# Moving 26 score maxima from the short sections to the front of a fused spectral-mix and attention kernel

## The chip, the cores and the metric

The kernel runs on one core of a Trainium2 chip. A core has a matrix engine (TensorE, PE in the profile, with its weight loads shown as PEld), a vector engine (VectorE, DVE), a scalar engine (ScalarE, ACT), GpSimd (POOL) and SyncE (SP), which here only issues transfers. They run at the same time, each through its own instructions in order, and wait for each other through semaphores. PE writes to PSUM, eight banks of 128 x 512 floats; ACT and DVE read them, GpSimd works on SBUF alone in this kernel.

The metric is the time of one execution in device microseconds (us), the median of several runs.

## The reference

For one input x (2048 x 512) the output is g * a + (1 - g) * b, with a gate per row, a two-dimensional Fourier transform a (its real part, by matrices), and attention b with 32 heads of 16 columns:

```python
g = sigmoid((x * gate_w).sum(-1, keepdims=True))
# a
ar = einsum("bsd,ed->bse", x, dft_hid_re);  ai = einsum("bsd,ed->bse", x, dft_hid_im)
a  = einsum("ts,bse->bte", dft_seq_re, ar) - einsum("ts,bse->bte", dft_seq_im, ai)
# b
q, k, v = split(x @ wqkv)                    # 32 heads of 16
p = softmax(q @ k^T * 16 ** -0.5)            # 2048 x 2048 for each head
b = (p @ v) @ wo
```

The inputs make the scores large, so softmax needs the maximum of each row of scores before the exponentials.

## The kernel before

Products are made in a rounded 32-bit type. Where precision matters a matrix is held as two parts, a rounded high part and a low part (the rest), and a product is the sum of three: high by high, high by low, low by high. `hi_lo` makes the parts: ACT copies the source into the high part, then DVE (or GpSimd, where the call says so and the source is in SBUF) subtracts.

Two heads form a *stack*: the high and low parts of q and k of a head lie in 64 partitions of `qs[p % 2]` and `ks[p % 2]`, the second head in the other 64. There are 16 stacks; two lie on the chip at a time. `load_stacks(p, heads)` (L267) fetches one from DRAM: for each head two fills with zeros and six rows of parts for p = 1 and 2, fewer fills later.

Scores are made twice. Once with the queries as rows, for their maxima: `a_tile(i, h)` (L288) makes one product of 128 queries by 512 keys for head h of stack i // 64, in a bank of PSUM (an "a"), and DVE reduces it to 128 maxima (L296). Each stack has 64 such i, each for two heads; 2048 maxima in all. When half a stack is done, `m_parts` and `m_rows` turn the maxima into two more rows of the queries, by way of DRAM. Then the scores proper, `scores(u, qb, h)` (L784, an "s"), come with the keys as rows and the maximum already subtracted; ACT makes the exponentials into `pt` (L801). A unit u is 128 keys by 1024 queries of one stack, four scores; there are 512 units. `pv` (L834) multiplies a unit with its values: four narrow products side by side, into the bank `acc`.

PE uses only 64 of its 128 rows for an "a" or an "s". The kernel therefore runs a second stream of products in the other 64 rows at the same time: products of the Fourier transform or of the output projection, each cut into two halves.

**The front.** First q and k (to 93 us), then v, then `b`, the imaginary half of the hidden transform. `pairs_of` (L400) makes the last eight tiles of v and all 16 tiles of b in groups of four. A group has four *phases* (L378): two pairs of tiles, each with its first and then its second half. A phase has 12 places, in each a half product of one tile beside one of the other; with `maxima` set, in places 3 and 9 two maxima (both heads) are put in between, which takes one more place. The first of the 24 phases makes none, 22 make four, until `a_next` has reached LEAD = 44. The second maximum of place 9 uses the bank `acc`, the others three banks in turn. When a pair has its second half, `done` empties it: `v_done` (L356) copies the two heads' columns into `vt`, one with ACT, one with DVE; `b_done` (L367) makes high and low parts in a tile `hl` of four buffers, stores them to `b_d` through SP, and for the first four tiles also makes the parts of the next weights (`wre`), the low ones on GpSimd.

**The main loop.** `segment` (L954) reads a pattern, one word for each place. "a" and "s" are a maximum and a score, with the number of the PSUM bank (0 to 6; 6 is `acc`), "-" is neither; a word with one letter also issues one half product of the second stream, a word with two letters puts two of the first kind side by side, and "|" is `pv` of one unit. There are two start sections (START), 13 pairs of short ones (THIN, 12 products of the second stream), 96 pairs of full ones (FULL, 16 products) and 13 pairs at the end (NINE, 9 products). A section pair makes the first half of its second-stream products, then the second half.

Before each section `run_plan` runs what is due: the plan (L882) is a list by units of values done. `load_stacks` for stack 1 is due at 0, the start of the loop; for stack p from 2 on the first head at 32 * (p - 1), the second two units later. The maxima of the main loop go on from `lead`, where the front stopped.

In the front, behind the transfers of `load_stacks`, SP issues the stores of `b_done`; in the main loop SP also issues the loads of the raw sequence matrices (`c_load`, L441), two buffers in turn, and the stores of values.

Of the kernel before, what the change touches and what calls it, by code (L numbers as in the profile page):

```python
# [9 lines left out]
F32 = mybir.dt.float32  # L10
F32R = mybir.dt.float32r
AF = mybir.ActivationFunctionType
ALU = mybir.AluOpType
AX = mybir.AxisListType

P = 128
S = 2048
D = 512
H = 32
DH = 16  # L20
NP = H // 2
KT = D // P
NT = S // P
UNITS = NP * 32
LEAD = 44
RAW = 6
PSUM = bass.MemoryType.PSUM
DRAM = bass.MemoryType.DRAM
# [3 lines left out]
def mix_kernel(ctx: ExitStack, tc: tile.TileContext, xa_t, xa, wqkv, w_hid, w_seq, wo, gate_w, out):  # L32
# [5 lines left out]
    nc = tc.nc  # L38
# [4 lines left out]
    used = list(range(7))  # L43
# [58 lines left out]
    acc = psO.tile([P, 512], F32, "acc")  # L102

    def hi_lo(hi, lo, src, lo_eng=None):
        nc.scalar.copy(hi, src)
        (lo_eng or nc.vector).tensor_tensor(lo, src, hi.bitcast(F32), ALU.subtract)
# [7 lines left out]
    st1 = right.__enter__()  # L114
# [9 lines left out]
    def staged(src):  # L124
        raw = st1.tile([P, D], F32, name="raw", bufs=RAW)
        i = nc.sync.dma_start(raw, src)
        if behind:
            tc.add_manual_dep(i.ins, behind.pop().ins.name,
                              mybir.DependencyInfo(mybir.DependencyClass.Sync, mybir.DependencyReason.DATA))
        return raw  # L130
# [58 lines left out]
    def bank():  # L189
        nonlocal banks  # L190
        banks += 1
        return (psS if banks % 2 else psA).tile([P, 512], F32, name="s" if banks % 2 else "a")


    with tc.tile_pool(name="qk", bufs=1, reuse_waits="tile") as pool:
# [38 lines left out]
        for tb in range(4):  # L234
# [4 lines left out]
            for c in range(2):  # L239
# [12 lines left out]
                for ct in range(4):  # L252
                    ps = bank()
# [9 lines left out]
    vt = main.tile([P, NT, NP, 33], F32, name="vt")  # L263
# [3 lines left out]
    def load_stacks(p, heads=range(2)):  # L267
        q_t, k_t = qs[p % 2], ks[p % 2]
        for h in heads:
            rows = slice((2 * p + h) * DH, (2 * p + h + 1) * DH)  # L270
            o = 64 * h
            if p:
                n = 64 if p < 3 else 50
                nc.sync.dma_start(q_t[o + 48:o + n].bitcast(F32), z_d[:n - 48])
                if p < 3:
                    nc.sync.dma_start(k_t[o + 50:o + 64].bitcast(F32), z_d[:14])

            for i, (qv, kv) in enumerate(((0, 0), (0, 1), (1, 0))):
                part = slice(o + 16 * i, o + 16 * i + 16)
                nc.sync.dma_start(q_t[part].bitcast(F32), qk_d[0][qv, rows])  # L280
                nc.sync.dma_start(k_t[part].bitcast(F32), qk_d[1][kv, rows])
# [6 lines left out]
    def a_tile(i, h, ps=None, bank=None):  # L288
        p, j = divmod(i, 64)
        qt, kb = divmod(j, 4)  # L290
        if ps is None:
            ps = psA.tile([P, 512], F32, "a", bank)
        r = slice(64 * h, 64 * h + (64 if p else 48))
        nc.tensor.matmul(ps, qs[p % 2][r, qt * P:(qt + 1) * P], ks[p % 2][r, kb * 512:(kb + 1) * 512],  # L294
                         start=True, stop=True)
        user = nc.vector.tensor_reduce(mx[p % 2][:, h, qt, kb:kb + 1], ps, AX.X, ALU.max)  # L296
        hf = j // 32
        a_left[p, hf] = a_left.get((p, hf), 64) - 1
        if not a_left[p, hf]:
            deferred.extend((partial(m_parts, p, hf), partial(m_rows, p, hf)))  # L300
        return user
# [45 lines left out]
    a_next = 0  # L347

    def x_mm(s, wh, wl):

        t = xab[s // 4][:, s % 4]
        for kt in range(KT):
            h1, l1 = (t[:, v, kt * P:(kt + 1) * P] for v in range(2))
            yield from ((h1, wh[kt]), (h1, wl[kt]), (l1, wh[kt]))

    def v_done(s, ps):  # L356
        pv = ps.rearrange("p (r h d) -> p r h d", h=2, d=DH)
        nc.scalar.copy(vt[:, s, :, 0:16], pv[:, :, 0])
        nc.vector.tensor_copy(vt[:, s, :, 17:33], pv[:, :, 1])
        if s in range(6, 14, 2):  # L360
            kt = (s - 6) // 2
            wt = st1.tile([P, 2, D], F32R, name="hl", bufs=4)
            hi_lo(wt[:, 0], wt[:, 1], wos.pop(0), nc.gpsimd)
            nc.sync.dma_start(wo_d[kt], wt.bitcast(F32))
            wrs.append(staged(w_hid[0, :, kt]))

    def b_done(s, ps):  # L367
        bt = st1.tile([P, 2, D], F32R, name="hl", bufs=4)
        hi_lo(bt[:, 0], bt[:, 1], ps)
        nc.sync.dma_start(b_d[s], bt.bitcast(F32))  # L370
        if s < KT:
            hi_lo(wre[0][s], wre[1][s], wrs.pop(0), nc.gpsimd)
# [3 lines left out]
    made, user = 0, None  # L376

    def phase(pair, half, maxima):  # L378
        nonlocal a_next, user
        before, user = user, None  # L380
        for j in range(12):
            for x, (ps, ops, done) in enumerate(pair):
                st, mv = ops[j]
                r = slice(64 * (half ^ x), 64 * (half ^ x) + 64)
                i = nc.tensor.matmul(ps, st[r], mv[r], start=not half and not j, stop=half == 1 and j == 11)  # L385
                if not j and not x and half:
                    tc.add_manual_dep(i.ins, before.ins.name,
                                      mybir.DependencyInfo(mybir.DependencyClass.Sync, mybir.DependencyReason.DATA))
            if maxima and j in (3, 9):
                for h in range(2):  # L390
                    used = a_tile(a_next, h, acc if h and j == 9 else None)
                user = user or used
                a_next += 1
        if half:
            for ps, ops, done in pair:
                done(ps)
        if deferred:
            deferred.pop(0)()

    def pairs_of(tiles, wh, wl, done):  # L400
        nonlocal made
        tiles = list(tiles)
        for i in range(0, len(tiles), 4):
            new = []
            for s in tiles[i:i + 4]:
                ps = psD.tile([P, 512], F32, name="d") if s % 4 == 1 else psS.tile([P, 512], F32, name="s")
                new.append((ps, list(x_mm(s, wh, wl)), partial(done, s)))
            for half in range(2):
                for pair in (new[:2], new[2:]):
                    phase(pair, half, 0 < made and a_next < LEAD)  # L410
                    made += 1

    for s in range(8):
        ps = psS.tile([P, 512], F32, name="s")
        ops = list(x_mm(s, *wv))
        for i, (st, mv) in enumerate(ops):
            nc.tensor.matmul(ps, st, mv, start=not i, stop=i == len(ops) - 1)  # L417
        v_done(s, ps)
    pairs_of(range(8, NT), *wv, v_done)

    def spare(i, dt, name):
# [4 lines left out]
    wre = [[const.tile([P, D], F32R, name=f"wre{v}{kt}", tag=f"w{4 * v + kt}") for kt in range(KT)] for v in range(2)]  # L426
    ab = [xab[s // 4][:, s % 4] for s in range(NT)]
    pairs_of(range(NT), *([w[:, kt] for kt in range(KT)] for w in (wch, wcl)), b_done)
    run_deferred()
    nc.vector.memset(acc, 0.0)  # L430
    assert a_next == LEAD
    right.__exit__(None, None, None)
# [420 lines left out]
    def take(gen, n, whole=True):  # L853

        got = []
        while len(got) < n:
            x = next(gen, None)
            if x is None:
                break
            x[0].left -= 1  # L860
            got.append((*x, x[0].left == 0))
            if whole and got[-1][4]:
                break
        return got
# [19 lines left out]
    def at(u, f, *args):  # L884
        plan.setdefault(u, []).append(partial(f, *args))
# [9 lines left out]
                    for step, du in enumerate((20, 24, 26)):  # L895
                        at(last + du + 8 * half, block, step, hf, ct, half)

    for p in range(1, NP):
        for h in range(2):
            at(32 * (p - 1) + 2 * h * (p > 1), load_stacks, p, [h])  # L900
    one, two, three = [(psD, "d")], [(psS, "s"), (psD, "d")], [(psS, "s"), (psA, "a"), (psD, "d")]
    side = [(psD, "d"), (psP, "a")]
    at(456, load_yg, 0, range(3))
# [8 lines left out]
    def run_plan(u):  # L912
        for v in sorted(v for v in plan if v <= u + 1):
# [8 lines left out]

    FULL = "a5 s4 a2 s0 a3 s6 a5 s4 s1 s0 s2 a6 a3 a4 s5 a1 | |"
    START = "sA s aS - - a s - - a s - - a", "s a s a s a s a s a s a +s +a"
    THIN = ("a2S4 a1 s3 a0 s6 s2 a4 s3 s1 a6 a0 s5 a2 s4A3 | |",
            "a2S4 a1 s3 a0 s6 s2 a4 s3 s1 a6 a0 s5 a2 s4A3 | |")
    NINE = ("a3 s0 s5 a4 a1 s6 s3 a0 a2 s5A4 | s5S1 a3A0 |",
            "a2S4 a5 s1 a3 s0 s6 a4 a1 s5S2 s0 a3 | s5A4 s1A2 |")

# [75 lines left out]
    def pairs():  # L1005

        for i in range(NT - 3):
            yield THIN, take(hid, 12)
        for i in range(2 * NT * 3):
# [131 lines left out]
```

## Time and profile before

| | us |
|---|---|
| median of 3 runs | 1657.53 (1657.33 to 1657.91) |
| the profiled execution's own time | 1657.73 |
| its span, first to last instruction | 1656.0 |
| granted TensorE clock (mean, of 1) | 0.999 |

The span by stage, from the starts of instructions in the trace:

| stage | from | to |
|---|---|---|
| q, k, and half of v | 0 | 115.2 |
| v and b in pairs, with maxima | 115.2 | 192.5 |
| two start sections | 192.5 | 205.5 |
| 26 short sections | 205.5 | 349.6 |
| 192 full sections | 349.6 | 1451.6 |
| the end | 1451.6 | 1656.0 |

A row of the timeline reads: start, length, engine, line, operation, tile written <- tiles read, shapes, count; in brackets the idle time of the engine before it and what ended it. A row of the view by lines reads: line, engine, operation, tiles, shapes, count, then busy time and the mean length of one in ns, then idle time before it. A row of the stretches gives from:to, length, and for PE, weight loads, DVE, ACT and GpSimd the busy time and the number of instructions. The length shown for one instruction is more than its share of time where the engine overlaps it with the next.

### The profile page before, as it was taken

Reading aid. Unit: us, or ns where it says so; the run is one execution under the profiler, and the core shown is the slowest. Engines: PE = TensorE matmul, PEld = TensorE weight load, DVE = VectorE, ACT = ScalarE, POOL = GpSimd, SP = SyncE. Lnnn points to the kernel's source line nnn. Section 1 sums busy time; section 2 is a strip of 40 time slices with the busy share of each in tenths; the row PEclk is TensorE's granted clock in tenths of the full one; section 3 lists DMA queues with packets and bytes.
Section 4 is the critical chain, followed back from the end, with each engine's and each line's share of the span. In section 5 each row is a group of like instructions: output and inputs, shape, how many; then the busy total and the mean of one; then the engine's idle time right before and its main releaser. Section 6 shows DMA issues by size and latency. Waiting matters only on the chain.

```text
span 1656.0 us, 34484 instructions
## 1 busy us (share of the span) xinstructions
PE 1648.4 (100%) x13082; PEld 990.4 (60%) x13082; DVE 1381.0 (83%) x2362; ACT 1259.6 (76%) x2469; POOL 654.0 (39%) x619
## 2 busy tenths in 40 slices
PE   9999999999999999999999999999999999999998
PEld 7888765555555555555555555555555555544454
DVE  5439888888888888888888888888888888899954
ACT  5212388888888888888788887888888887889996
POOL 0202133443434455444343455544434455333330
PEclk9999999999999999999999999999999999999999
DMA  9973610514151443414157434315141535452014
GB/s 291 348 166 109 186 20 9 70 34 85 46 91 47 74 113 81 95 46 79 47 90 255 92 115 95 87 59 92 47 91 56 116 104 119 139 186 47 25 44 142
DMA packets 85246, 167.16 MB, mean 101 GB/s; under 512 B 22460, under 2 KB 22716, under 8 KB 81068
## 3 DMA queue, kind: packets, MB, share of 16 engines
q1 hardware_dynamic: 84648, 164.30, 39.8%
q8 instruction: 103, 1.69, 0.5%
q10 hardware_dynamic: 432, 0.66, 0.1%
q14 instruction: 63, 0.52, 0.1%
HBM read 109.67 MB, written 55.17 MB: 100 GB/s over the span
## 4 chain that ended last, share of the span: by engine, by line
PE 99%; DMA 0%; DVE 0%; DVEq 0%; ACT 0%; SPq 0%; issue 0%
PE acc L846 28%; PE a L294 22%; PE s L800 19%; PE d L471 12%; PE s L385 3%; PE acc L800 3%; PE acc L294 2%; PE s L417 1%; PE d L385 1%; PE acc L808 1%; PE a L111 1%; PE a L110 1%; PE s L111 1%; PE s L110 1%; PE a L109 1%; PE s L109 1%
## 5 line engine op out<-in xcount | busy, mean ns | idle before, releaser
L296 DVE TENSOR_REDUCE mx<-a 128x1 f32<-128x512 f32 x1808 | 1127.8, 683 | 157.5 <-PE a L294 107.5
L801 ACT ACTIVATE pt<-s 128x512 f32<-128x512 f32 x1792 | 943.9, 628 | 15.1 <-PE s L800 11.1
L294 PE MATMUL a<-ks,qs 64*128 64x512 f32 (+1 forms) x1808 | 673.0, 408 | 0.0
L471 PE MATMUL d<-xab,ch 64*128 64x512 f32 x2016 | 648.1, 396 | 0.0
L800 PE MATMUL s<-qs,ks 64*128 64x512 f32 (+1 forms) x1792 | 591.5, 399 | 0.0
L828 POOL TENSOR_TENSOR oe<-oe,part 128x512 f32<-128x512 f32 x215 | 278.1, 1293 | 659.3 <-ACT part L827 654.3
L846 PE MATMUL acc<-pt,vt 128*17 128x512 f32 x3968 | 479.0, 595 | 0.0
L294 PEld LDWEIGHTS a<-ks,qs 64*128 64x128 f32 (+1 forms) x1808 | 322.2, 184 | 242.6 <-issue 133.1
L471 PE MATMUL d<-xab,cl 64*128 64x512 f32 x1008 | 399.3, 396 | 0.0
L471 PEld LDWEIGHTS d<-xab,ch 64*128 64x128 f32 x2016 | 366.6, 184 | 14.2
L800 PEld LDWEIGHTS s<-qs,ks 64*128 64x128 f32 (+1 forms) x1792 | 320.3, 184 | 81.0 <-ACT pt L801 29.8
L827 ACT COPY part<-acc 128x512 f32<-128x512 f32 x215 | 126.3, 588 | 202.2 <-issue 187.1
L846 PEld LDWEIGHTS acc<-pt,vt 128*17 128x17 f32 x3968 | 89.0, 96 | 228.2 <-issue 148.4
L471 PEld LDWEIGHTS d<-xab,cl 64*128 64x128 f32 x1008 | 185.6, 184 | 6.9
L296 DVE TENSOR_REDUCE mx<-acc 128x1 f32<-128x512 f32 x240 | 165.5, 690 | 11.4
L456 POOL TENSOR_TENSOR cl<-craw,ch 128x512 fp32r<-128x512 f32 x126 | 162.1, 1287 | 10.1
L801 ACT ACTIVATE pt<-acc 128x512 f32<-128x512 f32 x244 | 148.1, 607 | 0.0
L800 PE MATMUL acc<-qs,ks 64*128 64x512 f32 (+1 forms) x244 | 95.4, 391 | 0.0
L294 PE MATMUL acc<-ks,qs 64*128 64x512 f32 (+1 forms) x240 | 94.1, 392 | 0.0
L455 POOL CAST ch<-craw 128x512 fp32r<-128x512 f32 x126 | 77.1, 612 | 18.5 <-PE d L471 14.2
L471 PE MATMUL d<-wre,xab 64*128 64x512 f32 x336 | 83.0, 392 | 0.0
L471 PE MATMUL d<-wo_hl,o_hl 64*128 64x512 f32 x252 | 66.7, 395 | 0.0
(175 smaller groups left out, 1199.4 us busy)
## 6 DMA issues: line engine op xcount, KB each, us to landing
craw<-w_seq SPq DMA_DIRECT2D x128, 256.0 KB
qk<-hl SPq DMA_DIRECT2D x32, 512.0 KB
qs<-qk SPq DMA_DIRECT2D x96, 128.0 KB
ks<-qk SPq DMA_DIRECT2D x96, 128.0 KB
b<-hl SPq DMA_DIRECT2D x16, 512.0 KB
xab<-b SPq DMA_DIRECT2D x16, 512.0 KB
o<-oe SPq DMA_DIRECT2D x62, 128.0 KB
oh<-nh SPq DMA_DIRECT2D x12, 512.0 KB
```

The lines of the kernel that those rows point to most:

```text
L109: nc.tensor.matmul(ps, sh, mh, start=first, stop=False)
L294: nc.tensor.matmul(ps, qs[p % 2][r, qt * P:(qt + 1) * P], ks[p % 2][r, kb * 512:(kb + 1) * 512], start=True, stop=True)
L296: user = nc.vector.tensor_reduce(mx[p % 2][:, h, qt, kb:kb + 1], ps, AX.X, ALU.max)
L385: i = nc.tensor.matmul(ps, st[r], mv[r], start=not half and not j, stop=half == 1 and j == 11)
L455: nc.gpsimd.tensor_copy(h1, raw)
L456: nc.gpsimd.tensor_tensor(l1, raw, h1.bitcast(F32), ALU.subtract)
L471: i = nc.tensor.matmul(self.ps, st[r], mv[r], start=not self.begun, stop=stop)
L800: nc.tensor.matmul(ps, ks[p % 2][rr, kt * P:(kt + 1) * P], qs[p % 2][rr, q0:q0 + 512], start=True, stop=True)
L801: return nc.scalar.activation(pts[u][:, 2 * qb + h], ps, AF.Exp, bias=0.0, scale=DH ** -0.5)
L827: nc.scalar.copy(part[0], acc)
L828: nc.gpsimd.tensor_tensor(total, total, part[0], ALU.add)
L846: i = nc.tensor.matmul(acc[32 * j:32 * j + 17], v[:, 16 * h:16 * h + 17], pt[:, j], start=begin, stop=done or close)
```

## The change

- LEAD goes from 44 to 57. In `phase`, odd phases put maxima in at places 2, 6 and 10, even ones at 3 and 9, while `a_next` is below LEAD; the bank `acc` is used by the second head of every odd `a_next`. That is 13 more pairs of maxima in the front.
- Both THIN patterns have a new order and a new choice of banks: seven maxima, eight scores, one "-".
- `v_done` copies the second head with ACT for the eight tiles made in pairs; with DVE for the first eight as before.
- `b_done` copies the PSUM tile with ACT into a new SBUF tile `b` (two buffers), and GpSimd makes both parts from it.
- `load_stacks(1)` is called in the front after the tenth phase; the plan's calls for stacks 2 to 15 are due two units (one section) sooner.

```diff
-LEAD = 44
+LEAD = 57
...
-        nc.vector.tensor_copy(vt[:, s, :, 17:33], pv[:, :, 1])
+        (nc.vector.tensor_copy if s < 8 else nc.scalar.copy)(vt[:, s, :, 17:33], pv[:, :, 1])
...
         bt = st1.tile([P, 2, D], F32R, name="hl", bufs=4)
-        hi_lo(bt[:, 0], bt[:, 1], ps)
+        b = st1.tile([P, D], F32, name="b", bufs=2)
+        nc.scalar.copy(b, ps)
+        nc.gpsimd.tensor_copy(bt[:, 0], b)
+        nc.gpsimd.tensor_tensor(bt[:, 1], b, bt[:, 0].bitcast(F32), ALU.subtract)
         nc.sync.dma_start(b_d[s], bt.bitcast(F32))
...
-            if maxima and j in (3, 9):
+            if maxima and j in ((2, 6, 10) if made % 2 else (3, 9)) and a_next < LEAD:
                 for h in range(2):
-                    used = a_tile(a_next, h, acc if h and j == 9 else None)
+                    used = a_tile(a_next, h, acc if h and a_next % 2 else None)
...
                     made += 1
+                    if made == 10:
+                        load_stacks(1)
...
-    for p in range(1, NP):
+    for p in range(2, NP):
         for h in range(2):
-            at(32 * (p - 1) + 2 * h * (p > 1), load_stacks, p, [h])
+            at(32 * (p - 1) + 2 * h - 2, load_stacks, p, [h])
...
-    THIN = ("a2S4 a1 s3 a0 s6 s2 a4 s3 s1 a6 a0 s5 a2 s4A3 | |",
-            "a2S4 a1 s3 a0 s6 s2 a4 s3 s1 a6 a0 s5 a2 s4A3 | |")
+    THIN = ("a1S0 a2 a3 s5 s4 - a1 s0 s6 s5 s2 a3 a4 s0A1 | |",
+            "a1S0 a2 a3 s5 s4 - a1 s0 s6 s5 s2 a3 a4 s0A1 | |")
```

## The prediction

> **What bounds the kernel now.** I read the page's first part, then the busy time by stretch: the front's paired part, the two start sections, the 26 short sections (THIN in the code), the 192 full ones.
>
> ```profile
> span 1656.0 us, 34484 instructions
> PE 1648.4 (100%) x13082; PEld 990.4 (60%) x13082; DVE 1381.0 (83%) x2362; ACT 1259.6 (76%) x2469; POOL 654.0 (39%) x619
> ```
>
> ```profile
> core 0: us, PE busy (x) PEld busy (x) DVE busy (x) ACT busy (x) POOL busy (x), PEclk, DMA share, GB/s
> 115.18:192.48 77.30, 77.30 (x666) 62.88 (x665) 66.67 (x113) 14.21 (x30) 9.81 (x10) 1.00 0.36 129
> 192.48:205.54 13.06, 13.06 (x75) 9.80 (x73) 8.59 (x17) 7.98 (x17) 3.79 (x4) 1.00 1.07 238
> 205.54:349.56 144.02, 144.02 (x1145) 85.24 (x1144) 127.39 (x215) 123.15 (x247) 57.49 (x58) 1.00 0.23 34
> 349.56:1451.56 1102.00, 1102.00 (x9218) 642.26 (x9216) 973.19 (x1663) 899.01 (x1762) 508.67 (x473) 1.00 0.39 90
> ```
>
> PE is shown busy all the time in every stretch, so its share cannot tell where it waits; the length of a section can. A full section takes 1102.00 / 192 = 5.740 us, a short one 144.02 / 26 = 5.539. Both end in the same 16 value products; ahead of them a full section has 16 places, in which a half-array product of the transform runs beside a score or a maximum, and a short one 14. The timeline of one full section gives the price of a place:
>
> ```profile
> 414.46 0.50 PE L294 MATMUL a<-ks,qs 64*128 64x512 f32 x1
> 414.80 0.39 PE L800 MATMUL s<-qs,ks 64*128 64x512 f32 x1
> 415.04 0.39 PE L471 MATMUL d<-xab,ch 64*128 64x512 f32 x1
> ...
> 418.02 0.39 PE L471 MATMUL d<-xab,cl 64*128 64x512 f32 x1
> 418.06 0.39 PE L294 MATMUL a<-ks,qs 64*128 64x512 f32 x1
> 418.37 1.05 PE L846 MATMUL acc<-pt,vt 128*17 128x512 f32 x8
> ```
>
> From 415.04 to 418.02 lie 13 steps, 0.229 us each. Two places less should make a short section 5.740 - 0.46 = 5.28 us. It takes 0.26 more. Its timeline shows for what:
>
> ```profile
> 221.33 0.68 DVE L296 TENSOR_REDUCE mx<-acc 128x1 f32<-128x512 f32 x1
> 221.69 0.40 PE L800 MATMUL s<-qs,ks 50*128 50x512 f32 x1
> 222.06 0.13 PEld L846 LDWEIGHTS acc<-pt,vt 128*17 128x17 f32 x8 [0.25 <-DVE mx L296]
> 222.07 1.91 PE L846 MATMUL acc<-pt,vt 128*17 128x512 f32 x16
> 223.91 0.50 PE L294 MATMUL a<-ks,qs 48*128 48x512 f32 x1
> 224.44 2.49 DVE L296 TENSOR_REDUCE mx<-a 128x1 f32<-128x512 f32 x4 [0.64 <-PE s L800]
> 226.84 0.68 DVE L296 TENSOR_REDUCE mx<-acc 128x1 f32<-128x512 f32 x1
> 227.63 0.13 PEld L846 LDWEIGHTS acc<-pt,vt 128*17 128x17 f32 x8 [0.26 <-DVE mx L296]
> ```
>
> The value products write the bank `acc`, and in the short pattern the fifth maximum of the section ("a6") lies in that bank. The reduction of it ends at 221.33 + 0.68 = 222.01, and the weights of the value products follow 0.05 later; the next time it ends at 227.52 and they follow at 227.63. Between the two, DVE is a chain without a gap: value products 222.07, first maximum on PE 223.91, first reduction 224.44, four in 2.49 (one each 0.60 us back to back, the last lasting 0.68), the fifth until 227.52. So DVE, through that bank, sets the length of a short section, and PE has 0.26 us to give in each. In a full section no such loss is left to win.
>
> **The change, part by part.**
>
> *Short sections.* Seven maxima in place of eight, and one place ("-") in which the transform product runs alone; the places stay 14, so PE saves no place. What goes is the wait. In the new order `acc` holds a score ("s6", ninth place) and no maximum. I follow the new order from the start of one set of value products with the times above: places at 1.84 (223.91 - 222.07), then 0.34 later (414.46 to 414.80), then every 0.23: the ninth at 3.79, the last at 4.94, the value products 0.31 after the last (418.06 to 418.37) at 5.25; by the full section's own length 5.28, which I take. Against it the banks: reductions end 3.05, 3.65, 4.25, 4.85 (first start 2.37, 0.60 apart), so bank 1 is wanted again at 3.33 and free at 3.05; bank 3 wanted at 4.48, free at 4.25; bank 1 a third time at 4.94 ("A1" of the last place), free at 4.85. That is the tightest. ACT:
>
> ```profile
> 224.09 0.59 ACT L827 COPY part<-acc 128x512 f32<-128x512 f32 x1 [1.04 <-issue]
> 226.02 2.10 ACT L801 ACTIVATE pt<-s 128x512 f32<-128x512 f32 x4
> 227.93 0.67 ACT L487 COPY y<-d 128x512 f32<-128x512 f32 x1
> ```
>
> Exponentials come (2.10 - 0.62) / 3 = 0.49 apart, starting 2.5 after the value products. "s6" is the fifth, done at about 2.5 + 4 x 0.49 + 0.62 = 5.1, and `acc` is wanted at 5.28. Eight of them, the copy of `acc` and, every second time, the copy of y take 4.4 to 4.9 us of ACT; it does not bind at 5.28. Worth: 26 x (5.539 - 5.28) = **-6.7 us**. Bounds: nothing below 5.25 is possible for PE (-7.5); above, the wait of "A1" can cost the 0.11 that a restart costs over a step (0.34 against 0.23), 5.39, which leaves -3.9. I take 5.28, since the bank is free before it is wanted.
>
> *The front.* 13 pairs of maxima more (26 in all: places for 57 pairs and not 44). One pair is one place, both halves of the array:
>
> ```profile
> 155.97 0.39 PE L385 MATMUL s<-wch,xab 64*128 64x512 f32 x1
> 156.19 0.40 PE L294 MATMUL a<-ks,qs 48*128 48x512 f32 x1
> 156.20 0.40 PE L294 MATMUL acc<-ks,qs 48*128 48x512 f32 x1
> 156.43 0.40 PE L385 MATMUL s<-wcl,xab 64*128 64x512 f32 x1
> ```
>
> 0.23 from product to pair and 0.24 on to the next: 13 x 0.23 = **+3.0 us**, if nothing waits. The paired part's 77.30 us for 24 x 12 + 44 = 332 places are 0.233 a place, so it has at most 332 x 0.003 = 1 us of waits to win; I count none.
>
> DVE there: five pairs in two phases are 10 reductions, 6.0 us at 0.60, in 29 places, 6.7 us. It fits only because DVE gives up other work:
>
> ```profile
> L106 DVE TENSOR_TENSOR hl<-s,hl 128x512 fp32r<-128x512 f32 x10 | 6.6, 680 | 0.0
> L105 ACT CAST hl<-s 128x512 fp32r<-128x512 f32 x10 | 5.7, 589 | 39.8 <-PE d L385 17.4 <-PE s L385 12.1 <-issue 9.1
> L359 DVE COPY vt<-s 128x256 f32<-128x256 f32 x7 | 2.8, 418 | 2.4 <-ACT vt L358 2.3
> ```
>
> Sixteen subtractions of 0.68 go to GpSimd, eight copies of 0.42 to ACT. With both still on DVE it would have 66.67 + 26 x 0.60 = 82.3 us of work in 80.3. ACT has 14.21 us of work in 77.30; its eight copies (0.4 each) cost nothing. The copy it makes of a finished tile is as long as the rounded copy it made before, and now frees the PSUM bank by itself, 0.68 earlier.
>
> GpSimd gets, for each of 16 tiles, a rounded copy and a subtraction, at the prices of the same forms in the short sections:
>
> ```profile
> L828 POOL TENSOR_TENSOR oe<-oe,part 128x512 f32<-128x512 f32 x22 | 28.4, 1292 | 52.2 <-ACT part L827 52.2
> L489 POOL CAST xab<-y 128x512 fp32r<-128x512 f32 x13 | 7.9, 610 | 32.4 <-ACT y L487 32.4
> ```
>
> 1.9 us a tile, 7.6 for a group of four, whose four phases last 13.4. The first group has four subtractions of 1.29 for the real weights besides: 12.8. The new tile `b` has two buffers, so ACT's fourth copy of that group waits for the second tile's subtraction: counted from the end of the group's third phase 0.7 + 1.9 + 1.3 + 1.9 = 5.8, the copy done at 6.4, the bank wanted two phases on, at 6.7. Cost nothing, with 0.3 us of cover; behind that copy on ACT are only the next weight's copy and the next phase's tiles. Bounds: nothing, and with no cover at all once about 1 us.
>
> *The stacks.* Stack 1 is fetched after the tenth phase; its 16 transfers left SP here before:
>
> ```profile
> 140.27 0.42 SPq L126 DMA_DIRECT2D raw<-w_hid x1
> 152.04 4.86 SPq L370 DMA_DIRECT2D b<-hl  x4
> ...
> 194.88 0.68 SPq L274 DMA_DIRECT2D qs<-z  x1
> 207.50 0.30 SPq L281 DMA_DIRECT2D ks<-qk  x1
> ```
>
> SP is idle from 140.7 to 152.0, and the 13 us that the 16 issues took (194.9 to 207.8) end at 153.7 then; the first store of a finished tile waits behind them, and is ready about then (GpSimd's 2.6 us after 150). Its buffer of four is wanted a group later. Cost nothing. The fetch has to come early: maximum pair 64, stack 1's first, now falls into the second start section. The other 14 stacks go one section earlier, at a point where the scores that read the old stack have been issued; in SP's queue behind them stand loads of raw matrix chunks, two chunks (17 us) ahead of use. The full sections already stand at their 5.740; nothing to win, and no wait added. The start sections have the same orders and the same chains: 0 (between -0.3 and +0.2).
>
> **Sum**: -6.7 + 3.0 = -3.7. The profiled execution took 1657.73 us (span 1656.0 and 1.7 around it), 0.2 over the median 1657.53: 1657.73 - 3.7 = 1654.0, and 1653.9 beside the median.
>
> The Trainium skill ("Trainium Kernel Development and Optimization", Performance Expectations) says that the matmul busy share misjudges how much a kernel can still gain, because matmuls are pipelined. Read by the share, 100% in all four stretches, the wait in the short sections would not exist and the change would only add its 3.0; by the rule the share is no evidence, and the trace's 0.26 us between weights and reduction agrees with the rule.
>
> **Rivals.**
>
> *"A1" holds the sections up.* The short sections settle between 5.33 and 5.39: the bank is free only 0.09 before its place, and any lateness of DVE breaks the run of weights. For it: that small margin; against: nothing waits behind it but the value products, which need 0.31 anyway. 26 x 0.05 to 0.11 back: 1655.2 to 1656.8.
>
> *PE itself, or another engine, holds the short sections at 5.54.* For it: the busy share, and ACT's 123.15 of 144.02. Against: the 14 places by the full section's price, and ACT's 4.9. Then only the front's addition counts: 1657.53 + 3.0 = 1660.5.
>
> *Slower: GpSimd holds up the front.* Each PSUM bank is now freed by a copy into `b`, and each `b` by GpSimd; a late GpSimd stops ACT, then PE. At twice the rows' prices the first group needs 25.6 us for phases of 13.4 and the three others 15.2: up to 12 + 3 x 1.8 = 17 us, 1671. It decides from about 1.6 times the rows (12.8 x 1.6 - 13.4 = 7.1, which eats the 3.7 and 3.3 more). For it: two buffers and 0.3 us of cover in the first group. Against: these prices were taken beside a DVE busy 88% of the time.
>
> **How the numbers follow.** Forecast 0.60 (1652.8 to 1655.0), first rival 0.23, second 0.07, third 0.10. The range 1652.8 to 1657.2 holds the first two. A measurement of this kernel tells about 0.2%, 3.3 us: the line to faster is 1654.2, inside the forecast's own width; I give five sixths of the forecast to its far side, 0.50. Within: the rest of it, the first rival and the second, 0.40. Slower: 0.10.
>
> **What would show it.** Short sections 5.28 apart by the starts of their value products; their weights no longer waiting for a reduction; the paired front about 80.3 us; full sections still 5.740; GpSimd about 40 us busy in the front and ACT's copies never waiting for it to the point where PE stops. Wrong, if the short sections stay above 5.33 or the front grows by over 4 us.

## The result, and the profile after

| | before | after |
|---|---|---|
| median | 1657.82 us (22 runs) | 1655.51 us (22 runs) |
| ratio of after to before | | 0.9984, 95% interval 0.9979 to 0.9990 |
| the profiled execution's span | 1656.0 | 1653.7 |

The change is faster by 0.16%, 2.3 us; the interval allows 1.7 to 3.5 us. The forecast was 1653.9 with a range of 1652.8 to 1657.2: the time lies in the range, but not where the likeliest case had put it (1652.8 to 1655.0). It lies where the first rival had it (1655.2 to 1656.8). The prediction had given 0.50 to a time below 1654.2 and 0.40 to one within 0.2% of before; the second is what came.

The stretches of the changed kernel: the paired front, the start sections, the short and the full ones (from:to, length, then PE, weight loads, DVE, ACT, GpSimd busy with the number of instructions, granted clock, DMA share, GB/s).

```profile
114.81:195.21 80.40, 80.40 (x692) 71.99 (x691) 71.77 (x117) 16.67 (x38) 34.51 (x37) 1.00 0.55 147
195.21:208.26 13.05, 13.05 (x74) 9.85 (x73) 8.40 (x16) 8.08 (x17) 8.84 (x10) 1.00 0.41 162
208.26:347.08 138.82, 138.82 (x1119) 85.75 (x1118) 114.28 (x189) 124.98 (x246) 57.56 (x58) 1.00 0.18 29
347.08:1449.45 1102.37, 1102.37 (x9217) 637.69 (x9216) 972.60 (x1663) 899.35 (x1762) 508.85 (x473) 1.00 0.38 90
```

Set beside the stretches of before: the front 80.40 against 77.30, **+3.1**; the start 13.05 against 13.06; the short sections 138.82 against 144.02, **-5.2**; the full ones 1102.37 against 1102.00, +0.4. What lies before 115 us is 0.4 shorter and what lies behind the full sections 0.2 shorter, which no part of the change touches (in the thirteen traces of the table below the first of these is between 114.1 and 115.3 long). -0.4 + 3.1 - 5.2 + 0.4 - 0.2 = -2.3. A short section takes 138.82 / 26 = 5.339 us and not the 5.28 of the forecast: that difference times 26 is 1.5 us, nearly all of what the forecast was off.

One short section of the changed kernel, DVE and PE, shows where the 0.06 stays:

```profile
218.94 1.91 PE L851 MATMUL acc<-pt,vt 128*17 128x512 f32 x16
220.78 0.50 PE L294 MATMUL a<-ks,qs 64*128 64x512 f32 x1
221.32 4.43 DVE L296 TENSOR_REDUCE mx<-a 128x1 f32<-128x512 f32 x7 [0.76 <-PE a L294]
223.83 0.39 PE L805 MATMUL s<-qs,ks 50*128 50x512 f32 x1
223.86 0.49 PE L294 MATMUL a<-ks,qs 64*128 64x512 f32 x1
224.28 0.13 PEld L851 LDWEIGHTS acc<-pt,vt 128*17 128x17 f32 x8 [0.24 <-ACT pt L806]
224.28 1.91 PE L851 MATMUL acc<-pt,vt 128*17 128x512 f32 x16
```

The fourth reduction, of bank 1's second maximum, starts 221.32 + 3 x 0.60 and ends 0.68 later, at 223.80. The last place's maximum (the third in bank 1) begins at 223.86, 0.06 behind it, and the value products 0.42 after that, not the 0.31 of the forecast. The view of the waits, in the short sections, names the partner that is last to arrive, and it has changed (engine, tile and line <- releaser: us in all, times, longest), first of before, then of after:

```profile
PEld acc L846 <- DVE mx L296: 6.1, 25, 0.3
```

```profile
PEld acc L851 <- ACT pt L806: 6.1, 25, 0.2
```

The bank `acc` is now freed by an exponential, and that one has long ended (0.18 to 0.19 us before the value products). The wait shown is not the cause any more; it is only the last semaphore that the value products waited for. What holds the section stands one place ahead, at the last maximum, as the experiments show.

### The profile page after: what moved, and what is told of

Same layout as the page of the kernel before. It is cut to its first block, busy times and chain, and to the rows that moved or that the text cites. A ratio compares the mean times of both kernels' runs of the same rounds, so it can differ in the third digit from the quotient of the medians.

```text
span 1653.7 us, 34501 instructions
## 1 busy us (share of the span) xinstructions
PE 1646.4 (100%) x13082; PEld 995.5 (60%) x13082; DVE 1372.1 (83%) x2338; ACT 1264.0 (76%) x2477; POOL 683.8 (41%) x651
## 4 chain that ended last, share of the span: by engine, by line
PE 99%; DMA 0%; DVE 0%; DVEq 0%; ACT 0%; SPq 0%; issue 0%
PE acc L851 28%; PE a L294 23%; PE s L805 21%; PE d L476 9%; PE s L388 3%; PE acc L805 3%; PE acc L294 2%; PE s L422 1%; PE d L388 1%; PE acc L813 1%; PE a L111 1%; PE a L109 1%; PE s L111 1%; PE s L109 1%; PE a L110 1%; PE s L110 1%
## 5 line engine op out<-in xcount | busy, mean ns | idle before, releaser
L296 DVE TENSOR_REDUCE mx<-a 128x1 f32<-128x512 f32 x1828 | 1140.8, 683 | 164.0 <-PE a L294 103.1
L805 PE MATMUL s<-qs,ks 64*128 64x512 f32 (+1 forms) x1792 | 583.3, 397 | 0.0
L296 DVE TENSOR_REDUCE mx<-acc 128x1 f32<-128x512 f32 x220 | 151.8, 690 | 12.2
L294 PE MATMUL acc<-ks,qs 64*128 64x512 f32 (+1 forms) x220 | 85.8, 390 | 0.0
```

The costliest lines, as they stand in the source:

```text
L805: nc.tensor.matmul(ps, ks[p % 2][rr, kt * P:(kt + 1) * P], qs[p % 2][rr, q0:q0 + 512], start=True, stop=True)
```

## The experiments

Each is the changed kernel with one thing altered. Stage lengths come from the trace, between the first instructions of the stages; a short section is the median of the 26. All but before, after and e4 (ten) rest on one execution, and parts that an edit does not touch differ from run to run: 1.2 us ahead of the front, 1.2 us in the full sections. So the stages are to be compared, and spans that lie within 1 us of each other are not ranked.

| run | front | start | 26 short | one short | 192 full | span |
|---|---|---|---|---|---|---|
| before | 77.30 | 13.06 | 144.0 | 5.544 | 1102.0 | 1656.0 |
| after | 80.40 | 13.05 | 138.8 | 5.340 | 1102.4 | 1653.7 |
| e1_free_bank | 80.40 | 13.05 | 137.3 | 5.267 | 1102.2 | 1652.5 |
| e2_later_bank | 80.40 | 13.04 | 159.8 | 6.146 | 1101.7 | 1674.2 |
| e3_old_order | 80.40 | 13.05 | 144.2 | 5.556 | 1101.6 | 1658.6 |
| e10_max_in_acc | 80.49 | 13.05 | 151.8 | 5.830 | 1102.5 | 1667.3 |
| e4_dve_lows | 83.54 | 13.02 | 138.7 | 5.334 | 1101.4 | 1656.1 |
| e8_v_dve | 80.88 | 13.05 | 138.7 | 5.334 | 1101.3 | 1652.9 |
| e5_one_b | 92.70 | 18.49 | 138.8 | 5.340 | 1101.6 | 1670.7 |
| e11_three_b | 80.27 | 13.05 | 138.8 | 5.337 | 1101.8 | 1653.2 |
| e6_stack1_late | 80.49 | 19.22 | 141.7 | 5.335 | 1101.6 | 1661.2 |
| e7_stacks_late | 80.38 | 13.02 | 147.3 | 5.334 | 1102.0 | 1661.4 |
| e9_only_stack2 | 80.41 | 13.05 | 138.8 | 5.340 | 1102.0 | 1653.5 |

### What holds a short section

**The last maximum's bank set free.**

```diff
-        user = nc.vector.tensor_reduce(mx[p % 2][:, h, qt, kb:kb + 1], ps, AX.X, ALU.max)
+        if not skip[0]:
+            user = nc.vector.tensor_reduce(mx[p % 2][:, h, qt, kb:kb + 1], ps, AX.X, ALU.max)
+        else:
+            user = None
...
+                skip[0] = pattern in THIN and n == 6
```

`n == 6` is the seventh place.

> The changed kernel without the reduction of the second maximum that each short section puts in bank 1 (seventh place); the product itself stays, so PE has the same work and the last place's maximum finds its bank free. 26 reductions are left out, so the output is not the reference's. Theory W (the last place waits): the weights of the value products follow 0.48 us after the release of the bank that the last maximum wants, so without that wait the sections fall from 5.34 to between 5.25 and 5.29 us, about 1.5 us over the 26. Rival (PE's places, ACT or the lone product hold the section): it stays at 5.34.

The sections fell to 5.267, with PE's instructions unchanged: 137.29 for the 26, 1.5 us less. They alternate between about 5.26 and 5.31; why they do is not shown. Their mean is 5.280, so the wait of the last place cost the 0.06 that the forecast lacks, and 5.28 was right for PE's own places. The rows of the last maximum tell how, first of after, then of this run:

```profile
223.86 0.18 PEld L294 LDWEIGHTS a<-ks,qs 64*128 64x128 f32 x1
```

```profile
224.11 0.18 PEld L298 LDWEIGHTS a<-ks,qs 64*128 64x128 f32 x1
224.32 0.39 PE L298 MATMUL a<-ks,qs 64*128 64x512 f32 x1
224.64 1.91 PE L858 MATMUL acc<-pt,vt 128*17 128x512 f32 x16
```

In after the maximum does not start late: 4.93 behind the start of the value products, against 4.95 to 4.99 here. But its weights are loaded only when the bank is released, at the moment at which the product starts (223.86), and not 0.21 ahead; the product is 0.49 long and not 0.39, and the next step comes 0.42 later and not 0.32. This run also takes 26 reductions from DVE; the next one leaves DVE's work as it is.

**The same place, a bank that comes free later.**

```diff
-    THIN = ("a1S0 a2 a3 s5 s4 - a1 s0 s6 s5 s2 a3 a4 s0A1 | |", ...
+    THIN = ("a1S0 a2 a3 s5 s4 - a1 s0 s6 s5 s2 a3 a4 s0A5 | |", ...
```

> The changed kernel with the last maximum of a short section in bank 5 and not in bank 1. Bank 5 holds the tenth place's score, whose exponential ends 5.64 us after the start of the value products. Theory W: 5.64 + 0.48 = 6.12 us a section, 20 us more over 26. Rival (the switch to the value products, 0.31 us, hides a wait in the last place; they wait for the bank acc alone): below 5.45, with the value products starting when PE's places are through.

6.146, where 6.12 was expected. The timeline of one such section, the exponential of the tenth place's score and then PE:

```profile
231.99 0.63 ACT L806 ACTIVATE pt<-s 128x512 f32<-128x512 f32 x1
```

```profile
231.83 0.40 PE L805 MATMUL s<-qs,ks 50*128 50x512 f32 x1
232.68 0.50 PE L294 MATMUL a<-ks,qs 64*128 64x512 f32 x1 [0.45 <-ACT pt L806]
233.10 1.48 PE L851 MATMUL acc<-pt,vt 128*17 128x512 f32 x12
```

The exponential frees bank 5 at 231.99 + 0.63 = 232.62; the maximum follows about 0.05 later, the value products 0.48 after the release. The price is a sliding one: one place that waits moves the whole section by what its bank is late.

**The old order with one maximum less.**

```diff
-    THIN = ("a1S0 a2 a3 s5 s4 - a1 s0 s6 s5 s2 a3 a4 s0A1 | |", ...
+    THIN = ("a2S4 a1 s3 a0 s6 s2 a4 s3 s1 - a0 s5 a2 s4A3 | |", ...
```

> The changed kernel with the short sections' order and banks of before, but the maximum in acc (a6) replaced by a blank: seven maxima, none in acc. The prediction's reading (DVE through the bank acc sets the length): 5.28, or at least not above 5.34. Theory W: the last maximum (bank 3) waits for the exponential of the eighth place's score, 5.07 in the old order, so 5.07 + 0.48 = 5.55, as before the change: fewer maxima alone would bring nothing, the new choice of banks brings it.

5.556, as long as with eight maxima. DVE has its seven reductions, `acc` holds no maximum, and nothing is won: with the front's 3.1 the span is 1658.6, 2.6 over that of before. One section of it:

```profile
229.06 2.10 ACT L806 ACTIVATE pt<-s 128x512 f32<-128x512 f32 x4
```

```profile
230.23 0.40 PE L805 MATMUL s<-qs,ks 50*128 50x512 f32 x1
230.24 0.49 PE L294 MATMUL a<-ks,qs 64*128 64x512 f32 x1
230.66 1.91 PE L851 MATMUL acc<-pt,vt 128*17 128x512 f32 x16
```

The second of the four exponentials (0.48 after the first, 0.64 long) frees bank 3 at 230.18; the last maximum begins 0.05 later and the value products 0.48 after the release. So before the change there were two waits of nearly the same lateness, `acc` and the last place, and taking `acc` away alone does not shorten the section. The part of the change that earns the 5.2 us is the new choice of banks with the smaller number, not the smaller number. No run keeps eight maxima with other banks, so it stays open whether the smaller number, and with it the front's 3.1 us, is needed at all.

**A maximum in `acc` again.** Same number and order of maxima and scores as after the change, three banks moved.

```diff
-    THIN = ("a1S0 a2 a3 s5 s4 - a1 s0 s6 s5 s2 a3 a4 s0A1 | |", ...
+    THIN = ("a1S0 a2 a3 s5 s4 - a1 s0 s2 s5 s3 a6 a4 s0A1 | |", ...
```

> The changed kernel with the banks of three places changed, so that acc holds the twelfth place's maximum (a6) and no score; number and order of maxima and scores stay. Theory A (value products wait for the reduction of a maximum in acc, the first half of the prediction's reading): that reduction, the fifth, ends 5.6 to 5.9 us after the start of the value products, and they follow within 0.1: 5.7 to 5.95 us a section, 9 to 16 us more over 26. Theory W alone (only the last place's wait counts): the two tighter banks cost 0.1 to 0.2, 5.42 to 5.52.

5.830: the other half of the prediction's reading holds as well. DVE, then the weights of the value products:

```profile
266.32 0.69 DVE L296 TENSOR_REDUCE mx<-acc 128x1 f32<-128x512 f32 x1 [0.22 <-PE acc L294]
```

```profile
267.06 0.13 PEld L851 LDWEIGHTS acc<-pt,vt 128*17 128x17 f32 x8 [0.73 <-DVE mx L296]
```

The reduction ends at 267.01, the weights start 0.05 later.

### What the front costs

**DVE makes the low parts of b, as before.**

```diff
-        b = st1.tile([P, D], F32, name="b", bufs=2)
-        nc.scalar.copy(b, ps)
-        nc.gpsimd.tensor_copy(bt[:, 0], b)
-        nc.gpsimd.tensor_tensor(bt[:, 1], b, bt[:, 0].bitcast(F32), ALU.subtract)
+        hi_lo(bt[:, 0], bt[:, 1], ps)
```

> The changed kernel with the parts of the b tiles made by ACT and DVE from PSUM as before. By the count of DVE's work (71.9 us busy in the paired front, and 16 subtractions of 0.6 to 0.68 more: 81.5 to 82.8 in 80.2) DVE becomes the bound of the front: 1.5 to 3 us longer, 1657 to 1658.5, nothing gained over before. Rival (the four banks of maxima smooth it, or DVE's idle time at the start sections takes it): front 80.4, total unchanged within 0.5.

The front took 83.54, 3.1 more than after (1.5 to 3 were expected), and the total was 1658.26 us, 1.0007 of before (0.9998 to 1.0017): the whole gain is gone. DVE is the bound, but only in a part of the front; its work was expected at 81.5 to 82.8 and shows as 77.50 of 83.54:

```profile
114.95:198.49 83.54, 82.97 (x692) 66.80 (x691) 77.50 (x130) 16.39 (x38) 9.43 (x9) 1.00 0.53 146
```

From the twelfth phase on, where the first b tiles are finished, it works almost without a gap, and this part takes 47.08 us against 43.94 in after, the whole loss:

```profile
151.41:198.49 47.08, 46.51 (x379) 37.09 (x375) 46.83 (x81) 9.60 (x18) 5.56 (x6) 1.00 0.55 166
```

There the six phases with three pairs of maxima take 3.91 to 4.15 us each, and 3.48 to 3.49 in after, and the weights of the maxima wait for DVE:

```profile
PEld a L294 <- DVE mx L296: 2.5, 8, 0.5
PEld acc L294 <- DVE mx L296: 1.8, 6, 0.4
```

**The second copy of v back on DVE** (the last eight tiles).

> The changed kernel with both-heads copies of v as before (the second on DVE). In the paired v phases DVE then has per group of four 20 reductions of 0.60 and four copies of 0.42, 13.7 us, in phases of 13.4: front 0 to 0.7 us longer. Rival: DVE's start-up lag adds to it and the front grows by over 1 us.

80.88, 0.5 longer, within what was expected.

**One buffer for the tile b, and three.** `bufs=1` and `bufs=3` in place of 2.

> The changed kernel with one buffer for the tile b and not two. By the count of the prediction (GpSimd 1.9 us a tile, 1.3 more for the weights' low part in the first group of four) the fourth copy of the first group starts 9.1 us after the third phase's end, is done at 9.7, and its bank is wanted at 6.7: PE stands for about 3 us there (2 to 4), and nowhere else, since the later groups need 7.6 us of GpSimd for 13.4. Rival (GpSimd is no part of any chain that PE waits for): 0. Rival (GpSimd holds up the front in general): over 6.

> The changed kernel with three buffers for the tile b. The trace of the changed kernel shows the fourth copy of the first group done 0.04 us before its bank is wanted; if even that is no wait, front and total stay (80.4 us, 0 within 0.3). Rival (the two buffers already cost places in the first group's next phases): front 0.1 to 0.5 us shorter.

With three, the front is 0.13 shorter (80.27), but not at the place in question: the phase that ends there and the one that begins there take 3.27 and 3.49, in after 3.27 and 3.48. With one, the front grew by 12.3 and the start by 5.4, four times and more what was expected. The trace of that run has the expected stop, and what it sets off:

```profile
161.25 0.50 PE L388 MATMUL s<-wch,xab 64*128 64x512 f32 x1 [2.65 <-ACT b L370]
```

```profile
158.60:161.25 2.65, 0.01 (x2) 0.01 (x2) 0.52 (x1) 0.64 (x2) 2.57 (x4) 1.00 0.92 201
161.25:162.59 1.34, 1.34 (x12) 1.13 (x14) 0.31 (x1) 0.46 (x1) 1.26 (x3) 1.00 0.99 404
162.59:166.01 3.42, 3.42 (x20) 2.87 (x18) 2.27 (x4) 0.00 (x0) 2.40 (x2) 0.50 0.83 337
166.01:172.90 6.89, 6.89 (x63) 5.86 (x60) 6.42 (x12) 0.89 (x2) 2.33 (x4) 1.00 0.01 5
176.77:178.53 1.76, 0.00 (x0) 0.00 (x0) 0.65 (x2) 0.58 (x1) 1.09 (x1) 1.00 0.43 149
179.66:183.07 3.41, 3.41 (x20) 2.65 (x18) 2.49 (x4) 0.00 (x0) 0.85 (x1) 0.50 0.60 232
```

PE starts nothing between 158.10 and 161.25, the 3 us that were counted, and stands for 2.65 of them. Then, 1.34 us after it starts again, the granted clock (the third number from the end) falls to 0.50, for 3.42 us; at half the clock that is 1.7 us of work lost (an estimate from these two numbers). The three later groups stop too, against the expectation: two in the front, 1.76 us each, and the last in the start sections, 1.63 us. The expectation had set 7.6 us of GpSimd against 13.4 of phases, but what counts is when the fourth copy of a group is done. The four copies come one behind the other, the fourth is done some 8.6 us after the third phase's end, and its bank is wanted at 6.7. Each of these stops is followed by a time at half the clock, of 3.41 us in the front and 6.83 in the start sections. For the front 2.65 + 2 x 1.76 + 3 x 1.7 = 11.3 of the 12.3 us are so accounted for, for the start 1.63 + 3.4 = 5.0 of the 5.4.

### The stacks

**Stack 1 fetched at the start of the loop, as before.**

```diff
-                    if made == 10:
-                        load_stacks(1)
...
+    at(0, load_stacks, 1)
```

> The changed kernel with stack 1 fetched at the start of the main loop, as before. Its 16 transfers took SP 13 us there, behind the last stores of the front, which GpSimd now makes later; so the second head's rows land at about 214 to 216, and the first maximum that needs them is due at about 212, the first head's at 207.5. Expected: PE waits 3 to 6 us around the first short section. Rival: the rows land in time, 0.

The start took 19.22 (+6.2) and the short sections 141.7 (+2.8): 9.0 us, over the 3 to 6 expected. PE stands from 207.4 to 213.2, waiting for the stack's rows, and the granted clock is 0.50 from 209.7 to 216.5.

**Stacks 2 to 15 at their old times, stack 1 in the front.**

```diff
-            at(32 * (p - 1) + 2 * h - 2, load_stacks, p, [h])
+            at(32 * (p - 1) + 2 * h, load_stacks, p, [h])
```

> The changed kernel with stacks 2 to 15 fetched when they were before (two units later), stack 1 still in the front. Expected: full sections still 5.74, short ones 5.34, total within 0.5 us: this part of the change is worth nothing by itself. Rival (the earlier fetch wins or costs time in SP's queue): the full sections' sum moves by over 1 us.

A clear miss: the total rose to 1663.2 us, and the short sections to 147.25. All of it lies in two of them, the 19th and the 20th. The PE timeline there, then the stretches:

```profile
308.30 0.61 PE L476 MATMUL d<-wre,xab 64*128 64x512 f32 x2
314.35 0.76 PE L294 MATMUL a<-ks,qs 64*128 64x512 f32 x1 [5.43 <-DMA craw<-w_seq]
```

```profile
308.92:313.45 4.53, 0.00 (x0) 0.00 (x0) 0.00 (x0) 1.25 (x3) 1.58 (x2) 1.00 0.81 109
313.45:320.28 6.83, 5.93 (x25) 2.10 (x27) 2.02 (x5) 1.19 (x2) 0.00 (x0) 0.50 0.01 2
```

and SP's timeline of that run, first and last issue of the 16 for stack 2:

```profile
293.35 0.52 SPq L274 DMA_DIRECT2D qs<-z  x1
...
305.13 0.30 SPq L281 DMA_DIRECT2D ks<-qk  x1
```

The first maximum that needs the rows of the second head waits 5.4 us with PE idle, and the clock is at 0.50 for 6.83 us from 313.45 on. (The row names a load of the raw matrix. The semaphores that this product waits for in the trace are those of the second head's eight transfers, one of which that load uses again; the last to come is that of the transfer issued at 305.13.) The issues stood in SP's queue behind a store of finished values, which waited for GpSimd until 292. In after, where they are due one section earlier, the first head's eight leave at 283 to 286, ahead of that store, and the second head's at 293.7 to 297.4 and not at 297.9 to 305.4.

**Stack 2 alone one section sooner**, stacks 3 to 15 at their old times.

> The changed kernel with only stack 2 fetched one section sooner, stacks 3 to 15 at their old times. Without any of the earlier fetches two short sections (the 19th and 20th) took 8.5 us more, and no full section did. Theory S (the larger lead brings stack 2's first maxima so near to its fetch that one section decides): no section stands out, short sections 138.8 us, total as the changed kernel. Rival (the later stacks need it too, or the delay came from something else in that run): stalls remain at a stack's first maxima, over 2 us in all.

No section stands out: 138.8, span 1653.5. So it is the one stack that needs the earlier fetch.

## Why the prediction was right where it was, and where it was not

**The front: right.** +3.1 for 13 places at 0.23 (3.0). That DVE had to give up work was right, the way it was priced was not. The 82.3 us in 80.3 are for both shifts; with the 16 subtractions alone back on DVE the same sum gives 82.3 - 8 x 0.42 = 78.9, which fits into 80.3, and e4 lost 3.1 us all the same: the work is not spread over the whole front, and the part with the b tiles was over-full. The copies of v are worth 0.5 by e8. GpSimd was busy for 34.5 us in the front and not the 40 of the forecast; 5.05 us more than before fell into the start sections (8.84 against 3.79).

**The cover of GpSimd: right as a cost of nothing, too wide as a margin.** The prediction left 0.3 us. ACT's fourth copy of the first group, and the first product of the phase that wants its bank, in the trace of after:

```profile
157.39 0.59 ACT L370 COPY b<-s 128x512 f32<-128x512 f32 x1 [1.26 <-POOL hl L372]
```

```profile
158.02 0.51 PE L388 MATMUL s<-wch,xab 64*128 64x512 f32 x2
```

Done at 157.98, wanted at 158.02: of the 0.3 us 0.04 were left. One of the two products there even has its weights loaded only at 158.03, 0.05 behind the copy's end, and the next of its chain comes 0.34 later and not 0.23. It cost nothing that can be seen (e11), but the third rival was nearer than its 1.6 times; how much such stops cost one buffer less shows, 17.0 us on the span, as much as that rival's upper price.

**The short sections: the gain was mis-sized, by the term that the first rival had named.** "I take 5.28, since the bank is free before it is wanted": free at 4.85, wanted at 4.94. The bank was free at 4.86 and 0.06 was lost all the same, because a margin of 0.09 is too small to load the product's weights ahead; the value products come 0.48 after the release, so 4.86 + 0.48 = 5.34, and no later place hides it. e1 and e2 show that from both sides. The argument against the rival, that behind the last maximum stand only value products that need 0.31 anyway, is what failed: they came 0.42 after it. The prediction's own sign of being wrong, short sections above 5.33, came too, by 0.01.

**The reading of the wait: half of it.** "DVE, through that bank, sets the length of a short section". The bank does (e10, 0.05 from release to weights), but it was not alone: in the old order the last place's bank is as late, and with `acc` cleared e3 kept all 5.55. The prediction's second row shows it: a reduction that ends at 227.52 and weights at 227.63, 0.11 later, where 0.05 is what a release takes. In the trace of before it is 0.08 or more in 20 of the 26 short sections; there the last place (its bank released at 5.07, its maximum at 5.12, the value products at 5.55) was the later one, and in the other six, of 5.51 us, both come together. That the gain came was in part luck: the prediction did look at every bank of the new order, but it did not see that the last place of the old order was as late, so that to take the maximum out of `acc` would by itself have won nothing. The view of the waits names one partner, the one that came last. The second rival (PE or another engine holds the sections at 5.54) is out with 5.267 in e1.

**The stacks: the price of nothing was right for the change as a whole and wrong for the step.** "Nothing to win, and no wait added" was argued for the full sections, where it holds (1102.0 in e7). The step that failed is that the larger lead was not carried to the second stack: with 57 pairs made ahead and seven in two sections, where it was 44 and eight, stack 2's first maximum falls by the patterns into the 19th short section and no longer into the 20th, and the first that needs its second head, fetched last, into the 19th and no longer into the 21st, while the fetch was due where it had been; SP's queue does the rest. Without the earlier fetch the change would be 5 us slower than before (1661.4 against 1656.0). For stack 1 the prediction saw the need but no price; it is 9.0 us.

## What to carry to other kernels

When a section's length is set by a bank that comes free late, list for every place the time at which its bank is released against the time at which it is wanted, and look at the last places first: taking away one late bank shows nothing while a second is as late. A bank must be free long enough before its turn for the weights to be loaded ahead: here about 0.23 us, an estimate from the 0.05 between a release and the weight load and the 0.18 that the load takes. When work is moved ahead, follow everything that is timed by its progress, fetches above all, through the queue in which they stand.

## What the hardware showed that was not expected

A stop of PE costs more than its length. The granted clock in these traces is 1.00 or 0.50, and where it falls it stays at 0.50 for 3.41 us or twice that. In e5 it falls at 162.59, 179.66, 196.73 and 213.79, 17.07 apart, five times 3.41: so it seems to be set on a fixed beat, which would be why it fell 0.9 to 1.3 us after PE had started again in the front of e5, but in e6 and e7 while PE still stood. What PE did in the 3.41 us ahead of such a date tells whether it falls, here ahead of 179.66 in e5 and of 310.04 in e7, where it did not fall:

```profile
176.25:179.66 3.41, 1.65 (x16) 1.03 (x14) 1.26 (x3) 0.58 (x1) 2.57 (x4) 1.00 0.37 135
306.62:310.04 3.42, 2.29 (x18) 1.68 (x16) 2.28 (x4) 3.42 (x8) 3.34 (x4) 1.00 1.10 129
```

The six falls in e5, e6 and e7 each came after PE had been busy for 1.78 us or less of the 3.41 (1.34, 1.65, 1.65 and 1.78 in e5, 1.10 in e6, none in e7); after 2.29 in e7 and 2.35 in e6 there was none; where between 1.78 and 2.29 the bound lies is not shown. Stops of 0.45 us, one in every section of e2, left it at 1.00:

```profile
208.52:368.29 159.77, 148.23 (x1119) 85.70 (x1118) 117.38 (x190) 126.28 (x248) 57.66 (x58) 1.00 0.16 26
```

The Trainium skill ("TensorE: Matmul & The Clock Gate", Part 1) says that the array falls to half its clock after at least one idle window of about 3.4 us, and comes back after as long a busy one. The half clock agrees with the rows, and so does, in the front of e5, the length of the slow time; the idle window does not, since 1.6 us of standing within one of them was already enough.

Where a matmul waits for its bank, it starts about 0.05 us after the release, and its own weights are loaded no sooner; the next step then comes 0.42 later and not 0.31 when that is the value products.
